# The second product of a fused convolution and two-layer kernel, regrouped into tasks of 256 columns

## Chip, cores, metric

One core of a Trainium2 chip. The metric is device time in microseconds (us) for one execution.

## The reference

```python
# x: (8, 4096, 192), weight: (8, 7), w_in: (192, 2048), w_out: (2048, 192), all float32
w = softmax(weight, axis=-1)                       # 7 taps for each of 8 heads
out = einsum('hk,bskhg->bshg', w, x_unf)           # causal depthwise convolution over s
x = out.reshape(32768, 192)
h = x @ w_in
g = h * (1.0 / (1.0 + exp(-1.702 * h)))
return g @ w_out
```

## The kernel before

The kernel goes through 64 steps of 512 tokens. Each step has a *first product* (the convolved `x` times `w_in`) and a *second product* (`g` times `w_out`). The second product is a 2 x 2 block product done with seven block products in place of eight; each has 256 columns (tokens), 3 chunks of 32 output rows, and a contraction of 1024 in 8 pieces of 128. TensorE (PE) is used as four column tiles of 32, which work at the same time. Three chunks on four tiles is the awkward part; `before` cuts the 3 x 256 columns into six pieces so that every tile gets 192:

```python
TA = 3 * T // 4                     # 192
LANES = [                           # (column tile, chunk, first column, columns, place)
    (0, 0, 0, TA, 0),
    (1, 0, TA, T - TA, 0),
    (2, 1, T // 2, T // 2, 0),
    (3, 2, T - TA, TA, 0),
    (1, 1, 0, T // 2, T - TA),
    (2, 2, 0, T - TA, T // 2),
]
...
def product2(slot, bank, a, b, first=True):
    dst = slot[:, bank, 0:TA]
    for j in range(NK):             # 8
        for l, c, t, n, at in LANES:
            nc.tensor.matmul(
                dst[l * Q : (l + 1) * Q, at : at + n],
                w_out_s[:, a, j, c * Q : (c + 1) * Q],
                g[:, b, j, t : t + n], ...)
    return dst
```

Results go to PSUM *slots*: three tiles of two banks each, `slot[:, 0]` and `slot[:, 1]`, which first and second product share in rotation. VectorE (DVE) adds the products up and transposes them, ScalarE (ACT) copies and applies the activation:

```python
def output(s, last, work):
    ra, rb = last.x, last.z         # two of the three slots
    ...
    p1 = product2(ra, 0, A11, B11);  act.copy(u1, p1);  ...
    p3 = product2(rb, 0, S4, B22);   act.copy(u7, p3)
    work(2 if s > 1 else None)      # convolution pieces for a later step, on DVE
    c11 = product2(ra, 0, A12, B21, first=False);  turn(0, 0, c11);  work(2)
    p6 = product2(rb, 1, S2, T2);    vec.tensor_add(u2, u1, p6);  work(3)
    p7 = product2(ra, 1, S3, T3)
    p5 = product2(ra, 0, S1, T1)
    vec.tensor_add(u3, u2, p7);  vec.tensor_add(u1, u3, p5);  vec.tensor_add(u2, u2, p5)
    turn(1, 1, u1);  vec.tensor_add(u2, u2, u7);  turn(0, 1, u2)
    p4 = product2(rb, 0, A22, T4)
    vec.tensor_sub(u3, u3, p4);  turn(1, 0, u3)
    store(s, osb)
```

`prepare` is the list that `work(n)` takes convolution pieces from. In the main loop `a`, `b` and `nxt` are units of the first product, two to a step: their `p1` to `p7` are matmuls (others than those of the same names in `output`), `seed` and `keep` are copies on ACT, `add` are adds on DVE, `h` the activations on ACT:

```python
def prepare(big):
    ...
    for c in range(NC):
        for k in range(K):
            yield lambda c=c, k=k: conv(big, c, k)
    for i in range(4):
        yield lambda i=i: sums_c(big, i)
    yield lambda: cross(big)        # DMA f<-f
...
    work(6 if s > 1 else 9)
    a.add22(); a.h22(); a.p4(); a.h21()
    b.p1(); b.seed(); a.p3()
    work(2 if s == 1 else None if s % 2 else 4)
    a.add12(); b.p5(); b.p6(); ...; b.p7(); b.keep3(); b.h11()
    if nxt:
        nxt.p1()
    b.p5b()
    work(2); ...; b.add22(); b.p4(); ...; b.p3(); ...
    output(s, b, work)
```

## Time and profile before

| before | |
|---|---|
| median of 3 runs | 2475.07 us (2474.53 to 2476.35) |
| span of the profiled run, granted clock | 2474.9 us, 0.999 |
| matmuls of the second product, as the chip counts them | 43104 (672 a step) |
| second product, first product of a middle step | 18.61, 19.20 us |

"Second product of a step" here is the time on the PE timeline from the first matmul of its line to the first matmul of the next first product; "first product" is the rest of the step.

In the groups of the page (line, engine, operation, operands and count, then busy us and mean ns of one, then idle before them and what ended most of it) PE almost never idles:

```profile
L486 PEld LDWEIGHTS slot<-g,w_out_s 128*32 128x32 f32 x43104 | 1190.3, 110 | 35.2 <-issue 33.8
L486 PE MATMUL slot<-g,w_out_s 128*32 128x128 f32 (+2 forms) x43104 | 1208.2, 273 | 7.2 <-issue 6.1
L390 PE MATMUL slot<-f,w_in_s 64*128 64x256 f32 x7200 | 843.7, 376 | 0.4 <-DMA f<-f 0.2
```

The second product's matmuls (L486) wait 7.2 us in all. The first product's (L390) wait 0.4 us on this line; on the line of those that write the tile `sums`, which is not shown, they wait 2.8 us more. A change that adds a wait of PE therefore pays the whole of it.

### The profile page before, as it was taken

What the parts mean: (1) busy time and instruction counts of PE and PEld (TensorE: products, weight loads), DVE (VectorE), ACT (ScalarE), POOL (GpSimd) and SP (SyncE); (2) the same over time, 40 slices, a digit from 0 to 9 for tenths busy, and PEclk for the clock granted to TensorE, in tenths of its full rate; (3) what the DMA queues carried; (4) which work ended last, traced back from release to release, by engine and by line L of the source; (5) the groups of instructions that cost most, each with busy time, mean ns of one, the idle gap of its engine ahead of it and who ended that gap; (6) DMA issues with size and microseconds to landing.
All of it is one profiled execution on the core that took longest, in us unless ns stands there. A gap on an engine that the chain in (4) does not pass through costs nothing.

```text
span 2474.9 us, 114517 instructions
## 1 busy us (share of the span) xinstructions
PE 2454.8 (99%) x54434; PEld 2281.6 (92%) x54434; DVE 1701.4 (69%) x2348; ACT 941.2 (38%) x1052; POOL 8.1 (0%) x27
## 2 busy tenths in 40 slices
PE   9899999999999999999999999999999999999999
PEld 7799999999999999999999999999999999999998
DVE  8677666676666766666766667666676666677654
ACT  5333343343433433433434334334343343343342
POOL 1000000000000000000000000000000000000000
PEclk9999999999999999999999999999999999999999
DMA  7312122121221221221212212222122122121110
GB/s 178 66 37 59 36 56 58 29 57 40 52 58 32 56 55 37 58 46 40 58 40 53 58 32 55 47 45 57 37 50 58 36 56 50 37 58 40 28 35 16
DMA packets 197732, 123.58 MB, mean 50 GB/s; under 512 B 116048, under 2 KB 191440, under 8 KB 193296
## 3 DMA queue, kind: packets, MB, share of 16 engines
q1 hardware_dynamic: 196224, 115.32, 22.2%
q8 instruction: 425, 6.96, 1.2%
q0 software_dynamic: 288, 0.79, 0.1%
q14 instruction: 43, 0.35, 0.0%
q10 hardware_dynamic: 752, 0.16, 0.0%
HBM read 53.15 MB, written 25.17 MB: 32 GB/s over the span
## 4 chain that ended last, share of the span: by engine, by line
PE 98%; DVE 1%; issue 0%; DMA 0%; ACT 0%; SPq 0%; ACTq 0%; DVEq 0%
PE slot L486 49%; PE slot L390 31%; PE sums L390 18%; DMA f<-f 0%; DMA xin<-in_x_dram 0%; ACT g L413 0%; DVE f L353 0%; SPq L114 0%; DVE g L479 0%; DVE u L460 0%; DVE xt L336 0%; ACT u L430 0%; ACT u L443 0%; DVE osb L504 0%; DVE f L221 0%
## 5 line engine op out<-in xcount | busy, mean ns | idle before, releaser
L486 PEld LDWEIGHTS slot<-g,w_out_s 128*32 128x32 f32 x43104 | 1190.3, 110 | 35.2 <-issue 33.8
L486 PE MATMUL slot<-g,w_out_s 128*32 128x128 f32 (+2 forms) x43104 | 1208.2, 273 | 7.2 <-issue 6.1
L390 PE MATMUL slot<-f,w_in_s 64*128 64x256 f32 x7200 | 843.7, 376 | 0.4 <-DMA f<-f 0.2
L390 PEld LDWEIGHTS slot<-f,w_in_s 64*128 64x128 f32 x7200 | 692.8, 187 | 88.2 <-DVE u L460 1.8
L479 DVE TENSOR_TENSOR g<-g 128x1024 f32<-128x1024 f32 x504 | 600.2, 1222 | 191.5 <-ACT g L413 187.2
L390 PE MATMUL sums<-f,w_in_s 64*128 64x256 f32 x4080 | 511.9, 379 | 2.8 <-ACT u L443 2.8
L430 ACT COPY u<-sums 128x1024 f32<-128x1024 f32 x126 | 127.5, 1012 | 1004.6 <-PE sums L390 1004.6
L390 PEld LDWEIGHTS sums<-f,w_in_s 64*128 64x128 f32 x4080 | 390.4, 187 | 53.2 <-ACT u L443 4.4
L353 DVE SCALAR_TENSOR_TENSOR f<-xt,cw,f 128x512 f32<-128x512 f32 x564 | 421.9, 748 | 14.4
L413 ACT ACTIVATE g<-u 128x1024 f32<-128x1024 f32 x252 | 265.6, 1054 | 17.1 <-DVE u L470 14.4
L470 DVE TENSOR_TENSOR u<-u,slot 128x1024 f32<-128x1024 f32 x126 | 153.4, 1217 | 69.7 <-PE slot L390 69.7
L524 DVE TENSOR_TENSOR u<-u,slot 128x192 f32<-128x192 f32 x63 | 22.3, 354 | 247.6 <-PE slot L486 247.6
L460 DVE TENSOR_TENSOR u<-u,slot 128x1024 f32<-128x1024 f32 x126 | 153.2, 1216 | 54.2 <-ACT u L443 54.0
L443 ACT COPY u<-sums 128x1024 f32<-128x1024 f32 x126 | 127.5, 1012 | 128.4 <-PE sums L390 128.4
L413 ACT ACTIVATE g<-sums 128x1024 f32<-128x1024 f32 x128 | 130.4, 1019 | 94.7 <-PE sums L390 94.7
L413 ACT ACTIVATE g<-slot 128x1024 f32<-128x1024 f32 x132 | 135.4, 1027 | 49.8 <-PE slot L390 49.8
L423 ACT COPY sums<-slot 128x1024 f32<-128x1024 f32 x126 | 126.8, 1006 | 41.7 <-PE slot L390 39.7
L520 DVE TENSOR_TENSOR u<-u,slot 128x192 f32<-128x192 f32 x63 | 22.3, 354 | 93.2 <-PE slot L486 93.2
L514 ACT COPY u<-slot 128x192 f32<-128x192 f32 x63 | 20.1, 319 | 144.8 <-PE slot L486 144.8
L504 DVE STREAM_TRANSPOSE osb<-u 128x192 f32<-128x192 f32 x189 | 71.1, 376 | 4.3
L336 DVE STREAM_TRANSPOSE xt<-xin 128x576 f32<-128x576 f32 x96 | 67.1, 750 | 1.4 <-DMA xin<-in_x_dram 1.3
L531 DVE TENSOR_TENSOR u<-u,slot 128x192 f32<-128x192 f32 x63 | 22.3, 354 | 48.8 <-PE slot L486 48.8
(78 smaller groups left out, 317.1 us busy)
## 6 DMA issues: line engine op xcount, KB each, us to landing
xin<-in_x_dram SPq DMA_DIRECT2D x240, 180.0 KB, 4.3
f<-f SPq DMA_DIRECT2D x62, 576.0 KB, 4.8
out_dram<-osb SPq DMA_DIRECT2D x254, 48.0 KB, 1.7
out_dram<-osb SPq DMA_DIRECT2D x256, 32.0 KB, 1.6
out_dram<-osb SPq DMA_DIRECT2D x252, 16.0 KB, 1.5
g<-in_moe_w_in_dram SPq DMA_DIRECT2D x8, 384.0 KB, 9.2
g<-in_moe_w_out_dram SPq DMA_DIRECT2D x4, 768.0 KB, 5.2
xin<-in_x_dram SPq DMA_DIRECT2D x16, 160.0 KB, 3.0
```

The source lines that it names most:

```text
L336: vec.transpose(xts[big][:, c, :, :].rearrange("p n (j t) -> p (n j) t", t=Q), xins[big].rearrange("p n j d -> p (n j) d")[:, :, c * R : c ...
L353: vec.scalar_tensor_tensor(out=dst, in0=src, scalar=tap, in1=dst, op0=ALU.mult, op1=ALU.add)
L390: nc.tensor.matmul(slot[:, h, j * T : (j + 1) * T], w_in_s[halves[h], u, a, j * P : (j + 1) * P], f[halves[h], 0 if h == o else 1, b, :], ...
L413: act.activation(g[:, b, j : j + NK // NU, :].rearrange("p f t -> p (f t)"), src.rearrange("p h n -> p (h n)"), AF.Gelu_apprx_sigmoid,)
L423: act.copy(sums, self.x)
L430: act.copy(self.u2, sums)
L443: act.copy(self.u3, sums)
L460: vec.tensor_add(self.u3, self.u3, self.z)
L470: vec.tensor_add(self.u2, self.u2, self.z)
L479: vec.tensor_sub(v[dst], v[a], v[b])
L486: nc.tensor.matmul(dst[l * Q : (l + 1) * Q, at : at + n], w_out_s[:, a, j, c * Q : (c + 1) * Q], g[:, b, j, t : t + n], start=(first and j ...
L504: vec.transpose(osb[:, n, :, m * Q : (m + 1) * Q], src.rearrange("p (j t) -> p j t", t=Q),)
```

## The change

The intent is to ask PE for half as many, larger matmuls. Every task has 256 columns on each tile: tiles 0 to 2 take the three chunks of one product, tile 3 takes one chunk of another. Five products run this way; tile 3 does the sixth (`p3`, in tasks 1 to 3) and two chunks of the seventh (`p4`, in tasks 4 and 5). The last chunk of `p4` is shared: each tile does a quarter of its contraction (`quarters`), and DVE adds the four. A step has 336 matmuls in place of 672.

```diff
-    def product2(slot, bank, a, b, first=True):
-        dst = slot[:, bank, 0:TA]
+    def product2(slot, bank, ab, last, first=True):
+        dst = slot[:, bank, 0:T]
+        tiles = [(c, *ab, c) for c in range(NC)] + [(NC, *last)]
         for j in range(NK):
-            for l, c, t, n, at in LANES:
+            for l, a, b, c in tiles:
                 nc.tensor.matmul(
-                    dst[l * Q : (l + 1) * Q, at : at + n],
+                    dst[l * Q : (l + 1) * Q, :],
                     w_out_s[:, a, j, c * Q : (c + 1) * Q],
-                    g[:, b, j, t : t + n],
+                    g[:, b, j, :],
                     ...
-        return dst
+        return dst[0 : NC * Q, :], dst[NC * Q :, :]
+    def quarters(slot, bank, a, b, c):
+        dst = [slot[l * Q : (l + 1) * Q, bank, 0:T] for l in range(4)]
+        for i in range(NK // 4):
+            for l in range(4):
+                j = NK // 4 * l + i
+                nc.tensor.matmul(dst[l], w_out_s[:, a, j, ...], g[:, b, j, :], ...)
+        return dst
 ... (output, its end)
+        p5, p4c = product2(rb, 1, (S1, T1), (A22, T4, 0))
+        act.copy(chunk(p4, 0), p4c)
+        vec.tensor_add(u1, u2, p5)
+        vec.tensor_add(p3, u1, p3)
+        out.turn(0, 1, p3)
+        q = quarters(rb, 0, A22, T4, 2)
+        act.copy(chunk(p4, 2), q[2])
+        for l in (0, 1, 3):
+            vec.tensor_add(chunk(p4, 2), chunk(p4, 2), q[l])
+        p7, p4c = product2(ra, 0, (S3, T3), (A22, T4, 1))
+        act.copy(chunk(p4, 1), p4c)
+        vec.tensor_add(u1, u1, p7)
+        vec.tensor_add(u2, u2, p7)
+        out.turn(1, 1, u1)
+        vec.tensor_sub(u2, u2, p4)
+        out.turn(1, 0, u2)
 ... (main loop: b.p1 moves up in steps 1 and 2, which have no nxt.p1 yet to fill PE)
             a.p7()
+            b.p1()
             a.keep3()
 ...
-        b.p1()
+        if s > 2:
+            b.p1()
```

The stores and the first step's output are rewritten to the new layout; they play no part below, but for the 2.85 us that step 0 gains.

## The prediction

> **What bounds the kernel now.** I read the page's busy shares first, then the chain that ended last, then the groups, then the timeline of one step, then the waits.
>
> ```profile
> PE 2454.8 (99%) x54434; PEld 2281.6 (92%) x54434; DVE 1701.4 (69%) x2348; ACT 941.2 (38%) x1052; POOL 8.1 (0%) x27
> ...
> PE 98%; DVE 1%; issue 0%; DMA 0%; ACT 0%; SPq 0%; ACTq 0%; DVEq 0%
> ```
>
> TensorE is the bound: the chain is 98% PE. DVE and ACT cost time only where PE waits for them. The timeline of a step from the middle (64 steps, 63 of them alike), on PE:
>
> ```profile
> 1234.16 1.89 PE L390 MATMUL slot<-f,w_in_s 64*128 64x256 f32 x16
> 1235.98 9.29 PE L486 MATMUL slot<-g,w_out_s 128*32 128x192 f32 x330
> ```
>
> Line 390 is the first product, line 486 the second. Going from one L486 start to the next over the whole trace, I find a period of 37.80 us in an undisturbed step: 18.61 us of second product (1198.18 to 1216.79, 1235.98 to 1254.59, ...) and 19.2 us of first. PE never waits for another engine there. Some second products are longer, up to 19.76 us; the excess over 18.61 from the third step on sums to 9.5 us. The timeline marks such places so:
>
> ```profile
> 187.99 3.77 PE L486 MATMUL slot<-g,w_out_s 128*32 128x64 f32 x128 [0.20 <-issue]
> ...
> 101.36 5.39 PE L486 MATMUL slot<-g,w_out_s 128*32 128x192 f32 x184 [0.71 <-DVE osb L504]
> 109.05 4.80 PE L486 MATMUL slot<-g,w_out_s 128*32 128x128 f32 x104 [2.29 <-issue]
> ```
>
> They stand late in a second product (14 to 19 us after its start), never early, with no engine named: I read them as instruction supply running dry where 27.5 ns per matmul is asked. The first two second products take 23.71 and 23.89 us for that reason; after the 2.29 us gap the matmuls also run at 46 ns instead of 27.5. The wait of 0.71 us shows something else, used below: by source, PE was about to write the **second** bank of a PSUM slot, and waited for a DVE transpose that reads the **first** bank of that slot.
>
> **What the Trainium skill says.** "TensorE: Matmul & The Clock Gate", section "Wait — 56ns, not 53.3ns?": a warm matmul takes its columns at 2.4 GHz plus about 2.5 ns fixed. The trace agrees. An fp32 matmul is two instructions here (43104 for 21552 in the source), each at two cycles per column. The first product's 32 instructions of 256 columns, two at a time, take 3.45 us: 215.6 ns a round against 213.3 of pure streaming. In the second product a round (192 columns on each of four column tiles) is six matmuls; 255 instructions start in 7 us of the windows view, so 164.7 ns, against 160 plus two fixed costs on the tiles that take two pieces.
> "PSUM — Partial Sum Buffer", section "PSUM bank collisions raise a hardware error": no two of TensorE, VectorE and ScalarE may access a bank and quadrant at once, ACT against DVE reads included, so software must order them. The trace of before can only show PE against DVE (the 0.71 us); the built program of after shows that ACT and DVE reads of a bank are put in sequence.
> "VectorE: DVE Perf Modes", section on the TRN2 errata: an fp32 tensor_tensor takes (N+151)/0.96 ns. That gives 357 for 192 columns (trace 354) and 1224 for 1024 (trace 1217).
>
> **The change part by part.**
> (1) *Column work.* Before: 7 products x 8 chunks of contraction x 2 passes = 112 rounds of 192 columns. After: 5 x 8 + 2 = 42 tasks, so 84 rounds of 256. Both are 21504 columns per tile. Only the fixed cost shrinks: 84 x 215.7 ns = 18.12 us, plus about 0.15 us at the change of tiling (18.61 - 112 x 164.7 ns = 0.16) = 18.27. Gain 0.34 to 0.36 us a step, x63 = **-22 us**.
> (2) *Instruction supply.* Matmuls of the second product fall from 672 to 336 a step, and each asks supply at half the rate. I expect the dry spells to go: -9.5 us, about -5 of the 5.3 excess in the second step, and in the first step 96 rounds (20.7 us) plus 0.5 in place of 23.71: -2.5. **-17 us**.
> (3) *b.p1 earlier in the second and third step.* It fills the 1.16 us PE wait there with 0.86 us of work: **-1.7 us**.
> (4) *A new wait inside the second product.* The quarters task writes bank 0 of slot rb straight after the task p5 in bank 1 of rb. In the order of the built program with its waits, the first quarters matmul waits for the DVE add u1 = u2 + p5, which reads bank 1; the dependency goes by slot, as the 0.71 us showed. And that DVE add waits not for PE but for the ACT copy of the fourth tile of the same task. So PE idles for the whole relay. From the stream's end: ACT starts 0.25 us later (L510 copies begin at 1238.89, one product, 2.65 us, after 1235.98); the copy of 256 columns takes 0.322 + 64 x 0.83 ns = 0.375; DVE starts 0.03 after an ACT end (keep3 ended 75.82, the add began at 75.85); the add takes 0.354 + 64 x 1.04 ns = 0.42; PE restarts 0.05 after a DVE end (101.31 to 101.36), and 0.04 goes to the exposed weight load. Sum 1.17 us, x63 = **+74 us**.
> (5) *A new wait at the head of the next step.* The last task now is p7 in bank 0 of slot ra; before it was p4 in rb, and ra had long been read. The next step's first product writes sums (4 matmuls) and then p5 into ra. Count from T, the start of that first product. PE reaches ra at T+0.96 (1216.79 to 1217.75). A reader starts at T+0.11 (L531 at 1216.90): now ACT first, 0.375, then DVE at T+0.52, two adds that read p7, the second 0.336 later (L525 to L526 is 0.27 for 192 columns), ending T+1.27; PE restarts at T+1.32, plus 0.11 for the exposed weight load (after 75.87 the same group took 1.83 in place of 1.72). T+1.43 against T+0.96: 0.47, x62 = **+29 us**.
> (6) *DVE later in the next step.* After T, DVE now needs until T+2.35 for its tail; before 0.81. In odd steps it then runs six convolution pieces before add22, so h22, h21 and the seed copy on ACT end near T+10.9, where b.p6 needs sums at T+10.93 (10.46 plus the 0.47 of PE). With latency 0.12 x 31 = **+4 us**. In even steps add22 waits for keep3 anyway (33 such waits of 1.6 us), so nothing.
> (7) *End of the kernel:* one ACT copy and four longer DVE operations after the last matmul in place of two: **+1.4 us**.
> DVE's extra 2.4 us a step (ten adds of 0.42 and four transposes of 0.45, in place of six of 0.35 and four of 0.38) and ACT's extra 2 us are otherwise beside PE work, as DVE is at 69%.
> Sum: -22 - 17 - 1.7 + 74 + 29 + 4 + 1.4 = +67.7; rounded down a little for waits that may overlap: **2540 us**.
>
> ```profile
> ACT u L514 <- PE slot L486: 144.8, 63, 2.3
> ...
> DVE u L520 <- PE slot L486: 93.2, 62, 2.3
> ...
> DVE u L531 <- PE slot L486: 48.8, 63, 2.3
> ```
>
> These lines of the waits view show what the change spends: before, ACT and DVE wait for PE in the second product, every time, so they are never late. After, PE waits for them twice a step.
>
> **The rivals.** (a) *The waits are mild and the halved instructions win.* If the quarters wait did not hold PE (a bank of its own is written, and no data is shared), only (1), (2), (3), (5) would count: about 2464 us, 0.5% faster. If the wait at the step's head vanished as well, 2435. For it: the trace shows PE as the only bound. Against it: both waits stand in the built program, with the ACT copy in the relay, and the 0.71 us shows such a wait binding across banks. (b) *DVE or ACT becomes the bound.* DVE would go from 26.9 to some 29 us of a 39 us step: no, on the mean. But if the tail delays add22 enough to reach a.p3 too, or the seed chain is 0.4 us later than I count, odd steps cost 0.5 us more: 2555. (c) *The idle PE is clocked down.* A gap of 2.29 us was followed by half speed. The 1.16 us gaps at 75.87 and 121.25 were not, nor the 0.71 alone: I expect none, but a few such spells of 1.7 us would take the time above 2560. (d) *The four column tiles, of which one now streams other data, run slower or faster than 215.7 ns a round:* 1 ns is 84 x 63 = 5.3 us.
>
> **Range and chances.** The relay (4) is the largest term; each of its five parts is measured to about 0.03 us, so some 0.1 in all, 6 us. The head wait has the same uncertainty; supply and the odd steps 5 us each. That makes 2522 to 2556 for 8 in 10. The 2% line lies at about 2525: slower 0.85, within 2% 0.13, faster 0.02, the last for the case that both waits are hidden and supply stalls were worth more than I see.
>
> **What would show it right or wrong.** In the profile after: matmuls and weight loads of the second product down to 21552; a second product of about 19.4 us and a first product of about 19.7 in a middle step; the quarters line with idle of about 65 us in 63 waits, ended by the DVE add of p5; the first product into slots with some 22 us of idle ended by the DVE add of p7; "issue" waits nearly gone; PE busy down to some 96%. If the second product takes about 18.3 us, step (4) is wrong and the time is near 2465. If it takes 17.9 or less, the fixed cost per matmul was mis-sized. If the first product stays at 19.2, step (5) is wrong. If there is idle before sums at b.p6 of more than 0.3 us in odd steps, (6) is undersized.

## The result, and the profile after

| | before | after |
|---|---|---|
| median | 2475.11 us (2474.53 to 2476.35, 4 runs) | 2558.23 us (2558.13 to 2558.50, 4 runs) |
| span, granted clock of the profiled run | 2474.9, 0.999 | 2556.6, 1.0 |
| second product, middle step | 18.61 | 19.41 |
| first product, even / odd middle steps | 19.20 / 19.20 | 19.76 / 20.24 |
| second product of steps 0 and 1 | 23.71, 23.89 | 20.86, 19.41 |

The ratio is 1.0335 (95% interval 1.0317 to 1.0353): slower. Ratios here are the mean time of one kernel's fast runs over that of the other's of the same rounds, so not quite the ratio of the medians quoted.

The page of the changed kernel: the engines' busy time, the chain that ended last, and the groups.

```profile
PE 2466.2 (96%) x32882; PEld 1867.7 (73%) x32882; DVE 1847.1 (72%) x2600; ACT 1066.7 (42%) x1370; POOL 8.1 (0%) x27
...
PE 92%; DVE 4%; ACT 2%; issue 1%; DMA 0%; SPq 0%; ACTq 0%
...
L476 PE MATMUL slot<-g,w_out_s 128*32 128x256 f32 x20544 | 1133.3, 379 | 0.0
...
L379 PE MATMUL slot<-f,w_in_s 64*128 64x256 f32 x7200 | 875.5, 379 | 18.8 <-DVE u L567 18.3
...
L492 PE MATMUL slot<-g,w_out_s 128*32 128x256 f32 x1008 | 67.5, 385 | 59.0 <-DVE u L557 59.0
```

L476 is the five tasks of the second product, L492 the quarters, L379 the first product. The matmuls were halved (20544 + 1008 = 21552), their 6.1 us of idle that no engine ends are gone, and PE now waits for DVE twice a step: 59.0 us in all ahead of the quarters, 18.3 us at the heads of the next steps. In the chain DVE and ACT now have 6%, and PE has 92% where it had 98%. The timeline around the quarters of one middle step (start, duration, engine, line, operation; in brackets the idle before it and what ended it):

```profile
1244.53 0.61 PE L476 MATMUL slot<-g,w_out_s 128*32 128x256 f32 x8
1245.21 0.37 ACT L556 COPY u<-slot 32x256 f32<-32x256 f32 x1 [3.09 <-PE slot L476]
1245.61 0.42 DVE L557 TENSOR_TENSOR u<-u,slot 96x256 f32<-96x256 f32 x1 [0.80 <-ACT u L556]
...
1246.08 0.85 PE L492 MATMUL slot<-g,w_out_s 128*32 128x256 f32 x12 [0.94 <-DVE u L557]
```

This is a relay: PE ends task `p5`, ACT copies its fourth tile, only then DVE reads the other three, and only then PE may write the slot's other bank. The brackets say 0.94 us because the ends of matmuls are modelled; from start to start PE loses more: the quarters start 1.335 us after the last round of `p5` (1244.745, not printed), where a round takes 0.216, so 1.12 us. The same view 5 us later, where the next step's first product begins:

```profile
1250.53 1.13 PE L379 MATMUL sums<-f,w_in_s 64*128 64x256 f32 x8
1250.67 0.37 ACT L565 COPY u<-slot 32x256 f32<-32x256 f32 x1 [3.09 <-PE slot L476]
1251.07 0.42 DVE L566 TENSOR_TENSOR u<-u,slot 96x256 f32<-96x256 f32 x1 [2.14 <-ACT u L565]
1251.40 0.41 DVE L567 TENSOR_TENSOR u<-u,slot 96x256 f32<-96x256 f32 x1
...
1251.96 0.49 PE L379 MATMUL slot<-f,w_in_s 64*128 64x256 f32 x2 [0.29 <-DVE u L567]
```

The same relay with two adds; here PE has 0.97 us of other matmuls to do meanwhile, so less of it shows.

**Where 82 us went.** The 63 second products on the timeline sum to 1192.3 us before and 1224.4 after, the 64 first products to 1236.5 and 1284.2: +32.1 and +47.7 us, together +79.8 of the +81.7 between the spans (the rest lies in the last second product and the tail). The second products gained 2.85 and 4.48 us in steps 0 and 1 and lost 39.4 afterwards. The first products are unlike each other: +0.57 us in even steps, +1.05 in odd ones.

### The profile page after: what moved, and what is told of

Same layout as the page of the kernel before. It is cut to its first block, busy times and chain, and to the rows that moved or that the text cites. A ratio compares the mean times of both kernels' runs of the same rounds, so it can differ in the third digit from the quotient of the medians.

```text
span 2556.6 us, 71632 instructions
## 1 busy us (share of the span) xinstructions
PE 2466.2 (96%) x32882; PEld 1867.7 (73%) x32882; DVE 1847.1 (72%) x2600; ACT 1066.7 (42%) x1370; POOL 8.1 (0%) x27
## 4 chain that ended last, share of the span: by engine, by line
PE 92%; DVE 4%; ACT 2%; issue 1%; DMA 0%; SPq 0%; ACTq 0%
PE slot L476 44%; PE slot L379 31%; PE sums L379 15%; PE slot L492 3%; DVE u L557 1%; DVE u L566 1%; ACT u L556 1%; ACT u L565 1%; DVE u L567 1%; DVE f L342 0%; DMA f<-f 0%; DMA xin<-in_x_dram 0%; ACT g L402 0%; DVE u L449 0%; SPq L103 0%
## 5 line engine op out<-in xcount | busy, mean ns | idle before, releaser
L476 PE MATMUL slot<-g,w_out_s 128*32 128x256 f32 x20544 | 1133.3, 379 | 0.0
L476 PEld LDWEIGHTS slot<-g,w_out_s 128*32 128x32 f32 x20544 | 661.4, 110 | 450.7 <-issue 21.2
L379 PE MATMUL slot<-f,w_in_s 64*128 64x256 f32 x7200 | 875.5, 379 | 18.8 <-DVE u L567 18.3
L379 PEld LDWEIGHTS slot<-f,w_in_s 64*128 64x128 f32 x7200 | 758.5, 187 | 72.8 <-issue 42.1
L379 PE MATMUL sums<-f,w_in_s 64*128 64x256 f32 x4080 | 531.8, 380 | 1.3 <-ACT u L432 1.1
L379 PEld LDWEIGHTS sums<-f,w_in_s 64*128 64x128 f32 x4080 | 427.2, 187 | 46.9 <-issue 25.1
L449 DVE TENSOR_TENSOR u<-u,slot 128x1024 f32<-128x1024 f32 x126 | 153.4, 1218 | 33.1 <-ACT u L432 24.2
L412 ACT COPY sums<-slot 128x1024 f32<-128x1024 f32 x126 | 126.8, 1007 | 2.9 <-PE slot L379 0.7
L492 PE MATMUL slot<-g,w_out_s 128*32 128x256 f32 x1008 | 67.5, 385 | 59.0 <-DVE u L557 59.0
L566 DVE TENSOR_TENSOR u<-u,slot 96x256 f32<-96x256 f32 x63 | 26.3, 417 | 134.5 <-ACT u L565 134.5
L510 DVE STREAM_TRANSPOSE osb<-u 96x256 f32<-96x256 f32 x253 | 111.1, 439 | 7.3 <-DVE u L548 0.5
L557 DVE TENSOR_TENSOR u<-u,slot 96x256 f32<-96x256 f32 x63 | 26.3, 417 | 124.6 <-ACT u L556 124.6
L563 DVE TENSOR_TENSOR u<-u,slot 32x256 f32<-32x256 f32 x189 | 78.9, 417 | 45.7 <-ACT u L561 41.4
L565 ACT COPY u<-slot 32x256 f32<-32x256 f32 x63 | 23.1, 366 | 194.7 <-PE slot L476 194.7
```

The source lines that it names most:

```text
L379: nc.tensor.matmul(slot[:, h, j * T : (j + 1) * T], w_in_s[halves[h], u, a, j * P : (j + 1) * P], f[halves[h], 0 if h == o else 1, b, :], ...
L412: act.copy(sums, self.x)
L449: vec.tensor_add(self.u3, self.u3, self.z)
L476: nc.tensor.matmul(dst[l * Q : (l + 1) * Q, :], w_out_s[:, a, j, c * Q : (c + 1) * Q], g[:, b, j, :], start=(first and j == 0), stop=(j == ...
L492: nc.tensor.matmul(dst[l], w_out_s[:, a, j, c * Q : (c + 1) * Q], g[:, b, j, :], start=(i == 0), stop=(i == NK // 4 - 1), skip_group_check ...
L510: vec.transpose(self.osb[:, n, :, m * Q : (m + 1) * Q], src.rearrange("p (j t) -> p j t", t=Q),)
```

## The experiments

Three questions were open: do the two waits cost what their place says, what makes odd steps longer than even ones, and was it really the instruction rate that made `before` dry up? The built programs (order of instructions with their waits, no times) were checked first; the semaphores in the trace of the changed kernel agree with what is listed here:

```
first quarters matmul (bank 0 of rb)  waits for DVE L557 (reads bank 1 of rb)
DVE L557                              waits for ACT L556 (reads bank 1 of rb, fourth tile)
next step's first p5 matmul (ra)      waits for DVE L567 and for ACT L565
```

The first four kernels below ran together on one chip; `before` took 2472.46 us there (2467.37 to 2474.18, 7 runs), against 2475.11 where the changed kernel ran. Differences from the changed kernel's time are therefore checked against the step times of the traces.

### Quarters ahead of the reads of p5

The quarters' matmuls are issued before ACT and DVE read `p5`, so nothing reads the slot yet. The theory: PE then never waits there. The rival: PE needs the pause, or the readers that now start later make the next first product longer by as much.

```diff
         p5, p4c = product2(rb, 1, (S1, T1), (A22, T4, 0))
+        q = quarters(rb, 0, A22, T4, 2)
         act.copy(chunk(p4, 0), p4c)
         ...
-        q = quarters(rb, 0, A22, T4, 2)
```

> The matmuls of the quarters task are recorded before the ACT and DVE reads of p5, so the built order has no wait of PE between p5 and quarters; everything else as after. Theory (the wait is put on the whole two-bank slot, no data needs it): the gap of 1.12 us between the last round of p5 and quarters goes, the second product falls from 19.41 to 18.29 us, time about 2558 - 63 x 1.12 = 2488 us. The first product stays at about 19.76 (even) and 20.2 (odd). Rival (PE needs the pause for data, or the readers that now start 0.86 us later push the end of the step): second product shorter, but the first longer by as much, time above 2530.

Measured: 2486.67 us (2486.38 to 2486.68, 4 runs), ratio to before 1.0061 (1.0045 to 1.0078). The second product takes 18.27 us, the first products are as in the changed kernel (19.76, and 20.25 in odd steps). In the waits of this kernel (engine and line that waited, what it waited for, us, times, longest) no wait of the quarters for DVE is left, and the head wait stands as it was:

```profile
PE slot L379 <- DVE u L567: 18.4, 62, 0.3
```

So the relay cost 2558.2 - 2486.7 = 71.6 us by itself; the traces give 19.41 - 18.27 = 1.14 us a step, which is 72 us in 63 steps. A line moved up four places takes back 86% of the loss: the same matmuls, the same reads, the same slots.

### The first block of the exchange sent early

In odd steps `nxt.p1` reads block C11 from the half exchange. In the changed kernel DVE's tail after the second product is longer, so the convolution ends later and the exchange starts later. Timeline of an odd step after (SPq is the queue of the DMA issues):

```profile
1258.96 1.68 DVE L349 TENSOR_TENSOR f<-f 128x256 f32<-128x256 f32 x4
...
1260.70 1.11 SPq L355 DMA_DIRECT2D f<-f  x2
...
1265.03 2.11 PE L379 MATMUL slot<-f,w_in_s 64*128 64x256 f32 x15
...
1267.46 1.22 DVE L449 TENSOR_TENSOR u<-u,slot 128x1024 f32<-128x1024 f32 x1 [0.27 <-PE slot L379]
```

and of an odd step before:

```profile
1223.69 1.68 DVE L360 TENSOR_TENSOR f<-f 128x256 f32<-128x256 f32 x4
...
1225.42 1.11 SPq L366 DMA_DIRECT2D f<-f  x2
...
1230.70 1.89 PE L390 MATMUL slot<-f,w_in_s 64*128 64x256 f32 x16
```

Before, the exchange is issued 5.28 us ahead of the group with `nxt.p1` (1225.42 to 1230.70); after, 4.33 us (1260.70 to 1265.03), and the issues' table of the changed kernel gives 4.7 us from issue to landing. That group takes 2.11 us in place of 1.89. Then the DVE add that follows it (L449) is late, and so is what PE does after that add. The theory says that all of the odd steps' extra comes from this transfer. The rival is the prediction's own: the seed copy on ACT.

```diff
+    def conv_cross(big, c, k):
+        conv(big, c, k)
+        if c == 0 and k == K - 1:
+            cross(big, C11, C12)
 ...
-                yield lambda c=c, k=k: conv(big, c, k)
+                yield lambda c=c, k=k: conv_cross(big, c, k)
 ...
-        yield lambda: cross(big)
+        yield lambda: cross(big, C12)
```

> After, with the half-exchange transfer of f cut in two: the block C11, which is all that nxt.p1 reads, is sent as soon as its convolution is done, the rest as before. No DVE or ACT instruction moves. Theory (odd steps lose 0.45 us because nxt.p1 waits for that transfer, which starts later as DVE is later): odd first products fall from 20.23 to about 19.78 as even ones, time about 2558 - 31 x 0.45 = 2544 us, 0.5% faster. Rival (the seed copy or add22 on DVE and ACT are late by themselves, as the prediction counted): odd first products stay at 20.1 or more, time 2556 or more.

Measured: 2545.00 us (2544.89 to 2545.08, 4 runs), ratio to before 1.0298 (1.0282 to 1.0313). Odd first products fall from 20.24 to 19.78, even ones stay at 19.76; the second product stays at 19.41. In this kernel's waits, the two relays are unchanged (its lines stand five further down):

```profile
PE slot L497 <- DVE u L562: 59.1, 63, 0.9
...
PE slot L384 <- DVE u L572: 18.3, 62, 0.3
```

The transfer was the cause; nothing of the odd steps' extra but 0.02 us is left.

### Quarters last

The quarters go behind `p7`, so slots alternate: `p5` in rb, `p7` in ra, quarters in rb. The readers of `p5` then have the 3.4 us of `p7` to hide behind, and those of `p7` the 0.9 us of the quarters and the first matmuls of the next step. But the tail of ACT and DVE after the last matmul gets longer, which is a test of the chain that the prediction had in mind for odd steps.

```diff
-        q = quarters(rb, 0, A22, T4, 2)
-        act.copy(chunk(p4, 2), q[2])
-        for l in (0, 1, 3):
-            vec.tensor_add(chunk(p4, 2), chunk(p4, 2), q[l])
         p7, p4c = product2(ra, 0, (S3, T3), (A22, T4, 1))
         ...
         out.turn(1, 1, u1)
+        q = quarters(rb, 0, A22, T4, 2)   # and its copy and adds
         vec.tensor_sub(u2, u2, p4)
```

> Quarters moved behind p7, so that the tasks alternate between the two slots: p1 ra, p2 rb, p6 ra, p5 rb, p7 ra, quarters rb. Each slot's readers then have a task's time before PE writes the slot again, also at the head of the next step. Theory: both waits of PE go: second product 18.29, even first products 19.2 (from 19.76). But DVE now has the quarters' adds after the end, until 3.0 us into the next step in place of 2.35, so odd first products get worse, about 21 us: time 2558 - 71 - 17 + 24 = about 2494 us. Rival (the head wait was for the clock or for the change of tiling, not for readers of p7): even first products stay at 19.7.

Measured: 2491.97 us (2491.71 to 2492.09, 4 runs), ratio to before 1.0083 (1.0068 to 1.0098). Second product 18.27, even first products 19.19: both relays are gone. Odd first products rise to 21.01. The waits of this kernel say where:

```profile
PE slot L379 <- DVE u L449: 19.3, 30, 0.9
...
PE sums L379 <- ACT sums L412: 5.2, 31, 0.2
```

Here DVE's add22 (L449) and the seed copy (L412) do hold PE in odd steps, 0.64 and 0.17 us each. So the prediction's chain exists; in the changed kernel it was not yet long enough to bind. These two are 0.81 of the 1.82 us that odd steps have more than even ones. The starts of the matmuls tell where the whole of it goes (step 33 against step 32): 0.91 us is lost at `a.p3`, 0.44 at `b.p6`, 0.24 in the group with `nxt.p1` and 0.20 at `b.p3`. The last two places are those of the late exchange, but this run does not show that it is the cause here.

### Both waits gone, and DVE's work moved out of the odd steps' head

Quarters last, the first block sent early, and fewer convolution pieces ahead of add22 in odd steps (2 in place of 6): the second product of the even step before takes three of them, where DVE has time, and the later `work(None)` takes one.

```diff
 (quarters last and conv_cross as above, then)
-        work(2 if s > 1 else 3)
+        work(3)
-        work(2 if s > 1 else None)
+        work(3 if s > 1 else None)
-        work(3)
+        work(4)
 ... (main loop, ahead of add22)
-        work(6 if s > 1 else 9)
+        work(9 if s == 1 else 2 if s % 2 else 6)
```

> q_last and cross_early together, and three convolution pieces moved from the odd step's head into the even step's second product, where DVE has idle time. Theory: second product 18.29, all first products 19.2 to 19.3, no dry spells of instruction supply: before 2475 - 63 x 0.32 - 17 + about 2 at the end = about 2440 us, 1.4% faster than before. Rival (DVE as a bound, or the chain by ACT, still costs in odd steps): 2450 to 2470.

Measured: 2438.14 us (2437.96 to 2439.24, 4 runs), ratio to before 0.9866 (0.9852 to 0.9881): 1.3% faster than before, 4.7% faster than the changed kernel by the medians (2438.14 / 2558.23 = 0.953, on two chips). Second product 18.27 us in every step from step 1 on, first product 19.19 to 19.20 from step 3 on (but one of 19.42). The three parts were not tried in pairs, so the share of the moved convolution pieces is not shown by itself. One step on the PE timeline:

```profile
1210.58 1.90 PE L384 MATMUL slot<-f,w_in_s 64*128 64x256 f32 x16
1212.41 17.47 PE L481 MATMUL slot<-g,w_out_s 128*32 128x256 f32 x320
1229.70 1.05 PE L497 MATMUL slot<-g,w_out_s 128*32 128x256 f32 x16
1230.67 1.13 PE L384 MATMUL sums<-f,w_in_s 64*128 64x256 f32 x8
1231.64 1.89 PE L384 MATMUL slot<-f,w_in_s 64*128 64x256 f32 x16
```

The quarters (L497) follow without a bracket, and 1230.67 - 1212.41 = 18.26. The idea of the change was sound; what the changed kernel paid for was the order in which it was put.

### The same with half-size matmuls

Is it the number of matmuls, and not the new layout or the stores, that makes the dry spells go? On a second chip (before there: 2472.89 us, 2470.74 to 2474.29, 7 runs) the kernel of the last section ran with each 256-column matmul of the second product cut in two of 128. Data, order and stores are the same.

```diff
-        for j in range(NK):
+        for j, h in [(j, h) for j in range(NK) for h in range(2)]:
+            cols = slice(h * T // 2, (h + 1) * T // 2)
             for l, a, b, c in tiles:
                 nc.tensor.matmul(
-                    dst[l * Q : (l + 1) * Q, :],
+                    dst[l * Q : (l + 1) * Q, cols],
 ... (g likewise; quarters likewise)
```

> best, with every 256-column matmul of the second product split in two of 128 columns: twice the instructions (672 in a step, as before), same columns, same DVE, ACT and output transfers as best. Theory (a fixed cost of 2.3 to 2.6 ns per matmul in the chain of a column tile, and dry spells of instruction supply at 27 ns a matmul): rounds of 256 columns grow from 216 to about 219 ns, the undisturbed second product from 18.27 to about 18.5 us, and some second products are longer again by 0.2 to 1.2 us with gaps late in them that no engine ends, about 10 us in all past the second step and 3 to 7 us in the first two: time about 2438 + 14 + 14 = 2466 us. Rival (the dry spells of before came from its output transfers or from something else of before, not from the instruction rate): no such gaps, time about 2452. Second rival (issue has a floor near 27 ns that binds): rounds much over 220.

Measured: 2463.77 us (2460.73 to 2467.72, 4 runs), ratio to before 0.9966 (0.9949 to 0.9983). An undisturbed second product takes 18.48 in place of 18.27: 0.21 us over 84 rounds is 2.5 ns for each more matmul on a tile. And the dry spells are back: from step 2 on 14 second products are longer, by 6.7 us in all, and steps 0 and 1 take 22.39 and 21.63 (20.86 and 18.27 with whole matmuls). The group on this kernel's page, and two places on its PE timeline:

```profile
L482 PE MATMUL slot<-g,w_out_s 128*32 128x128 f32 x41088 | 1139.4, 273 | 5.1 <-issue 4.9
```

```profile
106.84 2.23 PE L482 MATMUL slot<-g,w_out_s 128*32 128x128 f32 x73 [2.77 <-issue]
...
144.27 3.70 PE L482 MATMUL slot<-g,w_out_s 128*32 128x128 f32 x128 [0.30 <-issue]
```

They look like those that the prediction showed of `before`: late in a second product, and no engine named. The queue table of the pages counts the transfers that bring instructions; before and after, and likewise split and whole, they follow the number of matmuls:

```profile
q8 instruction: 425, 6.96, 1.2%
```

```profile
q8 instruction: 257, 4.21, 0.7%
```

The first line is that of before (the split kernel has the same one), the second that of after (and of the kernel with whole matmuls). So it is the instruction rate, and the packed traces show the link itself. The gaps of over 0.1 us in second products that no engine ends are 14 in `before` and 8 in the split kernel. All of them begin at the same count of PE instructions modulo 256 (193 or 194, matmuls and weight loads counted in the order of their starts), and each ends 1.3 to 1.6 us after one of the q8 transfers, of 16,384 bytes, has landed. The expected 10 us past step 2 were 6.7. A side effect: kernels with 672 matmuls a step spread over 1.8 to 7 us from run to run (`before` 2474.53 to 2476.35 on one chip and 2467.37 to 2474.18 on another, split 2460.73 to 2467.72), those with 336 over 0.2 to 1.3 us.

### b.p1 in its old place

The kernel with both waits gone, with `b.p1` back where it was in steps 1 and 2 (one look, on the second chip).

```diff
-            b.p1()
             a.keep3()
 ...
-        if s > 2:
-            b.p1()
+        b.p1()
```

> best, with b.p1 of steps 1 and 2 put back to where before has it. Theory: without b.p1 in the wait for keep3, PE idles 1.16 us there again in both steps, in place of about 0.3; the first product of steps 1 and 2 grows from 21.42 and 20.63 to about 21.5 and 21.5 us, as part of what b.p1 saves in step 1 is lost to a later wait for the seed copy. Time plus 1 us, below what the times resolve; the trace is to show it. Rival: no difference in the first products of these two steps.

Measured: 2439.29 us, a single run of unknown state; a difference of 1 us cannot be told from times then. The timeline can tell: the first products of steps 1 and 2 take 21.51 and 21.49 us, against 21.42 and 20.63 with the move. It is worth 0.09 + 0.86 = 0.95 us.

### One engine to wait for at the head of the step

The head wait was 0.1 us longer than predicted, and PE restarted 0.15 us after the last DVE add ended (1251.81 to 1251.96), though 0.05 after that at the quarters (1246.03 to 1246.08). In the built program PE waits there for two engines. Here DVE does the copy that ACT did, so that one is left (on the changed kernel; checked in the built order).

```diff
-        act.copy(chunk(p4, 1), p4c)
+        vec.tensor_copy(chunk(p4, 1), p4c)
```

> The changed kernel with one line altered: the fourth column tile of the last task, p7, is copied out of its slot by DVE and not by ACT. In the built order the first matmul of the next step's p5 then waits for DVE alone, where it waited for DVE and ACT. Question: the head wait was 0.57 us where 0.47 was predicted, and the restart of PE after the end of the last DVE add took 0.15 us there (1251.81 to 1251.96) but 0.05 at the quarters. Theory A, a wait on two engines costs PE about 0.1 us more than a wait on one: DVE starts 0.11 us into the first product, takes three dependent operations at 0.33 us from start to start and 0.41 for the last, ends at 1.18, and PE restarts 0.05 later at 1.23 (1.43 in the changed kernel). The first product of even steps takes 19.56 us. Rival B, the 0.15 us belongs to that place (weights, bank, kind of matmul) whatever is waited for: restart at 1.33, even first product 19.66. The quarters wait and its 0.05 us stay in both. Odd first products fall by about 0.1 in both, as DVE's tail ends 0.1 earlier and the half exchange with it. Time 2549 for A, 2552 for B.

Measured: 2560.62 us (2560.37 to 2560.83, 4 runs), ratio to before 1.0342 (1.0325 to 1.0359), so not 9 us faster than the changed kernel, as theory A had it, but 2.4 us slower by the medians (on another chip; the intervals of the two ratios overlap) and by the spans of the two profiles. Its timeline at the head of a middle step:

```profile
1251.97 1.13 PE L379 MATMUL sums<-f,w_in_s 64*128 64x256 f32 x8
...
1252.11 0.43 DVE L565 COPY u<-slot 32x256 f32<-32x256 f32 x1 [1.74 <-PE slot L476]
1252.54 0.42 DVE L566 TENSOR_TENSOR u<-u,slot 96x256 f32<-96x256 f32 x1
1252.88 0.41 DVE L567 TENSOR_TENSOR u<-u,slot 96x256 f32<-96x256 f32 x1
...
1253.35 2.00 PE L379 MATMUL slot<-f,w_in_s 64*128 64x256 f32 x16 [0.24 <-DVE u L567]
```

The question it was made for has its answer: DVE ends at 1253.29 and PE restarts 0.06 later, against 0.15 in the changed kernel (0.055 and 0.147 in the median of 62 steps each). So at this place waiting for two engines cost some 0.09 us of restart (theory A); in the changed kernel's trace PE has an EVENT_SEMAPHORE instruction of its own for the second wait there, at 1251.86, and in this one none. The gain I had expected from it failed on another count. The copy is followed by the add after 0.43 us, not 0.33, so DVE ends 1.32 us into the first product and not 1.18, and even first products fall only to 19.71. Eight of them (one in four, at 20.0 us) are longer instead, and so is step 2 by 0.27; odd first products did not fall by 0.1, as expected, but rose from 20.24 to 20.28. Together this makes up the 2.4 us. The eight have a 0.2 us delay ahead of the last group of the first product, after a DVE add22 that began late. Why that add is late only there I have not followed up.

## Why the prediction was right and wrong

The direction, the mechanism and the largest terms held: 2540 was predicted, with slower at 0.85, and 2558 was measured, 2 us beyond the upper end of the range. Term by term, with the names of the prediction:

| term | predicted | shown by the runs |
|---|---|---|
| (1) column work | -22 | -21.4 (63 x 0.34: 18.61 to 18.27 without the relay) |
| (2) instruction supply | -17 | -17.6 (9.45 past step 1, 5.3 in step 1, 2.85 in step 0) |
| (3) b.p1 earlier | -1.7 | -0.95 |
| (4) relay before the quarters | +74 | +71.6 |
| (5) head wait | +29 | +35 (62 x 0.57) |
| (6) DVE later in odd steps | +4 | +13.2 (2558.23 - 2545.00; 31 x 0.48 would be 14.9, but the last odd steps lose less) |
| (7) the end | +1.4 | about +1, not measured by itself |
| sum | +67.7, rounded to 65 | +80.9; measured +83.1 (times from different chips) |

**(1)** Right to a hundredth: 18.27 us predicted, 18.27 measured as soon as the relay is gone. A round of 256 columns takes 216 ns with the fourth tile on other data, so rival (d) did not happen.

**(2)** Right in size, and its reason is now shown: with the same data and order, more matmuls bring the dry spells back. Not all of the 5.3 us in step 1 was waiting for instructions, though. The half speed after the 2.29 us gap, which the prediction noticed, was the clock: the trace of `before` has a granted clock of 0.5 from 109.94 to 113.35, which costs about 1.7 us.

**(3)** Right in kind, half in size. In step 2 the move saves 0.86 us, the full length of b.p1, but in step 1 only 0.09: there a wait of 0.17 us for the seed copy (ACT, L412) takes the place of part of the removed one. What took the rest there I did not follow; I had counted both steps alike.

**(4)** Right, and no story: moving one line removes exactly this term. The relay was 1.12 to 1.14 us against 1.17 predicted. That the wait binds across the two banks of a slot was read from one 0.71 us wait in the profile of before. That wait is no case of the rule on bank and quadrant that the prediction puts beside it, since write and read were in different banks; nor is DVE's wait for ACT in the relay, as the two read different quadrants (tiles 0 to 2, and tile 3). The recorded order is stricter than that rule. What a DVE add that does not wait for ACT would save was not tried.

**(5)** Mis-sized by 0.1 us a step, 6 us in all. The prediction took "PE restarts 0.05 after a DVE end" from a place with one wait; at the head of the step PE waits for ACT and DVE, and there it took 0.15. With one engine to wait for it took 0.06.

**(6)** This is the step that failed. The prediction said "In odd steps it then runs six convolution pieces before add22, so h22, h21 and the seed copy on ACT end near T+10.9", which would cost 0.12 us. The seed copy cost nothing that could be seen (0.01 us), and yet an odd step took 0.48 us more, 13 us in all and not 4. What the same delay of DVE did reach was a transfer: the half exchange left 0.95 us later against its reader, 4.33 us ahead of it and not 5.28, and it needs about 4.7. I had followed DVE's lateness through ACT to PE and not through the DMA queue to PE, though `nxt.p1` stands in the built program with a wait for that DMA. Rival (b) had named the right size (0.5 us in odd steps, 2555 us) but for the seed chain or a.p3; the run with quarters last shows that the seed chain and add22 do bind, only later, once DVE is later still. The sign that the prediction gave for this step ("idle before sums at b.p6") did not appear; the idle stood before nxt.p1 and b.p3.

Rounding 67.7 down to 65 "for waits that may overlap" was no good: nothing overlapped. Rivals (a) and (c) did not happen; after a gap of 0.94 us in every step the granted clock was 1.0. A gap of 2.77 us in the split kernel (ended at 106.84) was not followed by a lower clock either, unlike that of 2.29 us in `before`, so the length of the gap alone does not decide it. Rival (a) does describe the kernel with both waits removed, and its 2435 us is close to the 2438.14 measured there.

## What to carry to other kernels

When PE is the bound and idles nowhere, halving its instructions buys little (here 1.3%), and every new order of tasks must be read for what each task's first write waits for: two readers in sequence on one PSUM tile are a relay, and one line moved so that another task lies in between, or so that the write goes first, was worth 72 us. When an engine off the path gets later, follow its lateness into everything that it releases, transfers above all: see how long before its reader each transfer is issued and compare that with its time to landing. Restart times should be taken from a place with the same number of engines to wait for.

## What the Trainium skill lacked or had wrong

- "TensorE: Matmul & The Clock Gate", section "Wait — 56ns, not 53.3ns?": its fixed cost of about 2.5 ns a matmul was confirmed for fp32 and for four column tiles at once (0.21 us over 84 more matmuls a tile, 2.5 ns). The skill counts the passes of an fp32 matmul elsewhere, but no page says that it shows up as two instructions of two cycles a column, which is needed to reach the 216 ns a round of 256 columns seen here.
- "Runtime: NRT & Kernel Launch", section "Instruction fetch mechanics": it says that fetching is hidden because instructions are issued more slowly than they are fetched. For PE that did not hold: at 27.5 ns a matmul the supply ran dry for 9.5 us past the second step (17 second products) and for several us in the first two; at 54 ns a matmul, none. The split kernel shows it again with 6.7 us.
- "PSUM — Partial Sum Buffer": its rule on collisions is by bank and quadrant, and does not say that a tile of several banks can be ordered as a whole. In these kernels the order goes by the whole slot, and a write to one bank waited for reads of the other: 0.71 us once before, 1.12 us a step after. That lies in how the program is recorded and is no error of the page.
- No page gives what a wait of PE for two engines costs beyond a wait for one: restart 0.15 us after the end of the last add with two, 0.06 with one.
- No page says how long after the landing of its next block of instructions an engine that ran out of them goes on: in the 22 gaps counted under the half-size matmuls, 1.3 to 1.6 us.
